# Scaling far V on ScalarE, sharing q, k copies between two engines, and a later start of the rank work, in a fused attention and shrink kernel

## The chip, the core and the metric

The kernel runs on one core of one Trainium2 chip. A core has TensorE (PE, matmuls), VectorE (DVE), ScalarE (ACT), GpSimd (POOL) and SyncE (SP), each with its own instruction stream, and 16 DMA engines that move data between device memory (HBM) and on-chip memory (SBUF). Matmul results go to PSUM, which has 8 banks. The metric is the time of one execution on the device, in microseconds (us). A profiled execution also leaves a trace of every instruction.

## The reference

There are 4 batches, 8 heads, 768 positions and 64 values a head. Some heads ("retrieval") attend to all earlier positions, the others only to the first 4 positions (sinks) and the last 64. The attention's result, 3072 rows of 512, goes through two weight matrices with a shrink between them:

```
scores = q @ k.T / 8                       # per batch and head
mask   = causal & (retrieval | sink | rel < 64)
a      = softmax(where(mask, scores, -1e9))
x      = (a @ v), heads side by side       # 3072 x 512
h      = x @ w_in                          # 512 -> 2048
out    = (h - tanh(h)) @ w_out             # 2048 -> 512
```

The data type of the matmuls is FP16, sums are FP32. Which heads are retrieval heads is data, read on the chip.

## The kernel before, in words

The 3072 rows are cut into 12 tiles of 256 rows, three a batch. A tile's q and k come in, are put in head order as FP16 (`t16`), are transposed by PE (`st_T`, line 968, four 128x128 transposes for a pair of heads) into PSUM, and copied from there to `QK` (the copies of `st_T`, lines 949 on ACT and 951 on DVE). `st_S` (line 1042) adds the masks by a matmul (line 1052, tiles 0 and 1), makes the scores (line 1063), and has ACT take the exp (line 1076) into `pt`. `st_A` (line 1156) multiplies `pt` with V; DVE divides by the row sums (lines 1176, 1203) into `x16`, and `st_X` (line 1238) transposes the result into `xT`. `H_unit` makes 256 of the 2048 hidden columns of one tile: 16 matmuls (line 1267, two halves of 8), a tanh on ACT (1279), and h - tanh(h) on DVE into `gt` (1286). `O_group` multiplies `gt` with the second matrix (1325), ACT writes the result out of PSUM (1299).

V is held in two forms. `v1` is V as it is, used for the block of 128 keys on the diagonal and the one before. Farther keys count for streaming heads only if they are sinks, so for them V is multiplied per head and key by 0 or 1 (`vf`, "far V"). For batch 0 that is done by `scale_v` (line 715): one multiply a block of 128 keys, 128 x 8 x 65, on the engine named by `SV`. Tile 0 has the blocks 0 and 1, tile 1 the blocks 2 and 3 (tile 2's keys are never far). `vf` is first read by the weighting of tile 1.

The heads of batches 1 to 3 are put in an order of ranks, retrieval heads first. `by_rank` (line 835) works the ranks out by some 15 small DVE instructions (`iota`, `prod`, `cnt`, `pos`, `perm_i`, new masks `m4r`, `mS`); POOL then reads `perm_i` into registers and gathers heads with it. The list `LATE` names data that all these small instructions, but for the masks, wait for beside their own inputs; before, it is the result of the fourth head pair of tile 0 (`x16`, 3).

The order of all instructions is set ahead by a planner (`Plan`). Each step is registered with an engine, a planned duration, what it reads and writes, and, for a DMA, its packets; `Plan.run` steps through planned time and emits, engine by engine, the ready step that was registered first. The planner also gives out PSUM banks (scores take pairs of the banks 0 to 3 in the first part, everything else single banks 4 to 7), lets up to eight POOL DMAs be outstanding, and fills planned gaps of PE early on with dummy matmuls of 128 columns (line 1482). So a changed planned duration moves instructions although nothing of the work is changed, and the order, once emitted, is fixed: an engine that waits for one instruction holds all behind it.

POOL issues in this order: V of tile 0, q and k of tile 1, V of tile 1, the four quarters of the first matrix (line 603), the first quarter of the second (614), a select that finishes a part of the mask `mS` (736), then V, q and k of tile 2 with the far V multiplies (725) between them, another quarter of the second matrix, and the raw data of tile 3.

Of the kernel before, what the change touches and what calls it, by code (L numbers as in the profile page):

```python
# [12 lines left out]
TT = 256  # L13
# [3 lines left out]
class Plan:  # L17
# [28 lines left out]
    def op(self, eng, ns, fn, r=(), w=(), dma=None, prio=None, port=False):  # L46
        i = len(self.ops)
        deps = set()
        for k in r:
            if k in self.writer:  # L50
                deps.add(self.writer[k])
            if k[0] in self.PSUM:
                deps.update(j for j in self.readers.get(k, ()) if self.ops[j][0] != eng)
            self.readers.setdefault(k, []).append(i)
        for k in w:
            if k in self.writer:
                deps.add(self.writer[k])
# [12 lines left out]
        return i  # L70
# [185 lines left out]
def kernel(  # L256
# [111 lines left out]
    ORDER = ("t1", "v1", 0, 1, 2, 3, 4, "t2", 5, "r3", 6, 7)  # L368

    def program(first):  # L370

# [111 lines left out]
        def load_v(t):  # L483

            b, g = divmod(t, NG)
            for i in range(NB):
                blk = g * NB + i
                dma(
                    "POOL", 900,
                    lambda i=i, blk=blk: nc.gpsimd.dma_start(  # L490
                        out=v1s[b]()[:, blk, :, 0:D],
                        in_=v[b, :, blk * 128 : blk * 128 + 128, :].rearrange("h p d -> p h d"),
                    ),
                    128 * H, 15.5, w=[("v1", b, blk, x) for x in range(2)],
                )

        def load_cast(t):

            b, g = divmod(t, NG)
            batch(b)  # L500
            c, ic = t16s[t] = buf("t16")
            if t >= FROM:
                c5 = lambda: c()[:].rearrange("p (i x h d) -> p i x h d", i=NB, x=2, h=H)
                for i in range(NB):
                    s0 = g * TT + i * 128
                    for x, src in enumerate((q, k)):
                        dma(
                            "POOL", 900,
                            lambda i=i, x=x, src=src, s0=s0: nc.gpsimd.dma_start(
                                out=c5()[:, i, x, :, :],  # L510
                                in_=src[b, :, s0 : s0 + 128, :].rearrange("h p d -> p h d"),
                            ),
                            128 * H, 15.5, w=[("t16", ic, x, i, s_) for s_ in range(H)],
                        )
# [5 lines left out]
            for x, src in enumerate((q, k)):  # L520
                dma(
                    "POOL", 950,
                    lambda x=x, src=src: nc.gpsimd.dma_start(
                        out=pk()[:].rearrange("p (x h e) -> p x h e", x=2, h=H)[:, x, :, :],
                        in_=src[b, :, g * TT : (g + 1) * TT, :].rearrange(
                            "h (p i) d -> p h (i d)", i=2
                        ),
                    ),
                    128 * H, 22.6, w=[("t16p", ip, x)],
                )  # L530
            if t == 1 and first:
                return
            in_order(t)
            load_v(t)

        def in_order(t):

            (pk, ip), (c, ic) = packed[t], t16s[t]
            for x in range(2):
                op(  # L540
                    "DVE", 500,
                    lambda x=x: nc.vector.tensor_copy(
                        out=c()[:].rearrange("p (x i h d) -> p x i h d", x=2, i=2, h=H)[:, x],
                        in_=pk()[:].rearrange("p (x h i d) -> p x i h d", x=2, h=H, i=2)[:, x],
                    ),
                    r=[("t16p", ip, x)] + (BEHIND if t == 1 and first else []),
                    w=[("t16", ic, x, half) for half in range(2)], port=True,
                )

        def turn(t, i):  # L550

# [166 lines left out]
        def scale_v(t, eng="POOL"):  # L718
            b, g = divmod(t, NG)
            lo = g * NB  # L720
            for jb in range(lo, min(lo + NB, 4)):
                fl = rflag0 if jb == 0 else rflag
                op(
                    eng, {"DVE": 690, "POOL": 1053}[eng],
                    lambda jb=jb, fl=fl: engs[eng].tensor_mul(
                        out=vfs[b]()[:, jb, :, :], in0=v1s[b]()[:, jb, :, :],
                        in1=fl[:].unsqueeze(2).to_broadcast([128, H, D + 1]),
                    ),
                    r=[("v1", b, jb, 0), ("v1", b, jb, 1), "rflag0", "rflag"],
                    w=[("vf", b, jb, 0)], port=True,  # L730
                )

        def select(m, src, fill, base, step, mult, key, cmp=ALU.is_ge):
# [608 lines left out]
        def visits(t):  # L1342
            g = t % NG
            gen = [t * HP + hp for hp in range(HP) if not is_near(t * HP + hp)]
            near = [t * HP + hp for hp in range(HP) if is_near(t * HP + hp)]
            if near:
                a, c = gen
                d, e = near
                return {
                    0: [[(a, 0), (d, 0)], [(c, 0), (e, 0)]],  # L1350
                    1: [[(a, 0), (a, 1)], [(d, 0), (c, 0)], [(c, 1), (e, 0)]],
                    2: [[(a, 0), (a, 1)], [(a, 2), (d, 0)], [(c, 0), (c, 1)], [(c, 2), (e, 0)]],
                }[g]
# [153 lines left out]
        def spread_over(fs, lo, hi):  # L1507
            for i, f in enumerate(fs):
                plan.setdefault(max(0, int(lo + (hi - lo) * i / max(len(fs), 1))), []).append(f)

        if first and fast:
            spread_over([by_rank], BR, BR)
        spread_over(att_pairs(1) + [lambda: scale_v(1, SV)], 0, 0)
        spread_over(attention(2), *A2)
        between = {}

        def point(h):
            t, ts = divmod(h, 2)
            return slot_of[t, 4 * ts + 3] if t >= 2 else max(0, 13 + 2 * h)
# [36 lines left out]
                spread_over(attention(t), lo, hi)  # L1556

        for s, what in enumerate(slots):
            if first and fast and s == point(2 * NG * FLEX - LEAD - 1):
                P.split = len(P.ops)  # L1560
            fs = plan.get(s, [])
            mid = (len(fs) + 1) // 2
            for i, x in enumerate(what):
                for f in fs[:mid] if i == 0 else ():
                    f()
                if x[0] == "H":
                    H_unit(*x[1:])
                else:
                    t, ts, f0, f1, c0, c1 = x[1:]
                    O_group(t, ts, f0, f1, c0, c1)  # L1570
                for f in fs[mid:] + between.get(s, []) if i == 0 else ():
                    f()
# [59 lines left out]
```

## Time and profile before

| | us |
|---|---|
| median of 3 runs | 232.07 (231.43 to 232.75) |
| the profiled execution | 233.06 |
| its span, first to last instruction | 231.3 |
| PE busy | 221.7 (96% of the span) |
| VectorE busy | 146.7 |
| ScalarE busy | 139.9 |
| GpSimd busy | 97.5 |
| mean granted TensorE clock | 0.990 |

A row of the timeline gives the start, the time to the end of the last of the instructions merged in it, the engine, the line, what is written and read, shapes, the count, and in brackets the idle time of the engine before it with what ended it. A stretch (from:to) gives its length, the busy time and count of instructions of each engine, the granted clock, the DMA share and GB/s. A busy PE isn't PE at its peak, since matmuls overlap.

### The profile page before, as it was taken

To read this page: it belongs to the slowest core of one execution; us is meant where nothing else is said; L and a number is where in the kernel's file an instruction comes from. 1 tells how busy PE (TensorE), PEld (TensorE's weight loads), DVE (VectorE), ACT (ScalarE), POOL (GpSimd) and SP (SyncE) were. 2 spreads that over 40 slices of the span, in tenths; PEclk is the share of its full clock that TensorE was granted. 3 is DMA by queue.
4 is the path that set the end of the run, shared out by engine and by line. 5 is a ranking of instruction groups with operands and counts; after the bars stand their busy time and mean duration, and the time that the engine had idled before them with its cause. 6 is when DMAs were issued, how large, how long until landed. Compare 5 with 4: busy or idle time off the path is not lost.

```text
span 231.3 us, 6135 instructions
## 1 busy us (share of the span) xinstructions
PE 221.7 (96%) x2328; PEld 158.7 (69%) x2328; DVE 146.7 (63%) x355; ACT 139.9 (60%) x214; POOL 97.5 (42%) x231
## 2 busy tenths in 40 slices
PE   7879999989999999999999999999999999999992
PEld 6446788768887666766776676765957767766652
DVE  5878887893774766755774776466867547534400
ACT  3817837975566858747547756846875867534420
POOL 8998361980281918684363968280000000000000
PEclk9988999999999999999999999999999999999999
DMA  6999999979999999999979999944121211220112
GB/s 171 150 194 206 186 223 217 208 114 204 198 202 233 195 197 233 206 198 209 248 149 252 222 250 185 212 117 114 48 45 48 60 34 45 67 47 28 48 63 80
DMA packets 102964, 35.31 MB, mean 153 GB/s; under 512 B 90642, under 2 KB 100114, under 8 KB 102930
## 3 DMA queue, kind: packets, MB, share of 16 engines
q1 hardware_dynamic: 85632, 27.14, 56.3%
q0 software_dynamic: 17152, 7.60, 25.1%
q8 instruction: 19, 0.31, 0.6%
q14 instruction: 15, 0.12, 0.2%
q10 hardware_dynamic: 146, 0.13, 0.2%
HBM read 27.26 MB, written 6.29 MB: 145 GB/s over the span
## 4 chain that ended last, share of the span: by engine, by line
PE 84%; DVE 6%; DMA 3%; POOL 2%; ACT 2%; issue 1%; POOLq 0%; DVEq 0%
PE banks L1325 36%; PE banks L1267 34%; PE banks L1063 7%; PE banks L1156 6%; DMA t16p<-in_k_dram 3%; DVE gt L1286 2%; DVE pt L1117 2%; ACT pt L1076 1%; DVE prod L846 1%; POOL v L490 1%; PE banks L968 1%; PE banks L1052 1%; ACT th L1279 1%; DVE QK L951 0%; POOL A L736 0%
## 5 line engine op out<-in xcount | busy, mean ns | idle before, releaser
L1267 PE MATMUL banks<-xT,win 128*128 128x256 f16 x768 | 95.0, 273 | 0.7 <-DVE gt L1286 0.5
L1325 PE MATMUL banks<-wout,gt 128*128 128x512 f16 (+1 forms) x464 | 94.5, 343 | 1.1 <-DVE gt L1286 1.1
L1286 DVE SCALAR_TENSOR_TENSOR gt<-th,banks 128x512 f16<-128x512 f32 x96 | 65.1, 682 | 31.5 <-ACT th L1279 30.7
L1267 PEld LDWEIGHTS <-win 128*128 128x128 f16 x768 | 72.8, 98 | 15.5 <-issue 2.1
L1279 ACT ACTIVATE th<-banks 128x512 f32<-128x512 f32 x96 | 57.1, 601 | 40.5 <-PE banks L1267 39.4
L1076 ACT ACTIVATE pt<-banks 128x768 f16<-128x768 f32 (+1 forms) x60 | 52.9, 920 | 17.3 <-PE banks L1063 16.4
L1325 PEld LDWEIGHTS <-gt 128*128 128x128 f16 x464 | 43.0, 98 | 29.3 <-DVE gt L1286 1.3
L636 POOL CAST t<-rawqk 128x256 f16 x72 | 28.6, 443 | 30.6 <-DMA rawqk<-in_k_dram 14.7
L1299 ACT ACTIVATE ot<-banks 128x512 f32<-128x512 f32 (+1 forms) x28 | 15.0, 535 | 22.0 <-PE banks L1325 21.2
L1188 DVE TENSOR_TENSOR x16t<-banks,rinv 128x128 f32 (+1 forms) x80 | 22.9, 288 | 1.8 <-DVE x16t L1188 0.2
L1099 DVE TENSOR_TENSOR ptn<-ptn,mS 128x512 f16<-128x512 f16 x24 | 10.9, 493 | 17.0 <-ACT ptn L1076 17.0
L1063 PE MATMUL banks<-QK 64*128 64x128 f16 (+1 forms) x364 | 21.4, 241 | 0.0
L672 POOL CAST v<-rawv 128x128 f16 x72 | 19.7, 320 | 0.0
L1063 PEld LDWEIGHTS <-QK 64*128 64x128 f16 x364 | 12.7, 95 | 9.9 <-issue 6.8
L1076 ACT ACTIVATE ptn<-banks 128x1024 f16<-128x1024 f32 (+1 forms) x18 | 17.2, 953 | 3.8 <-PE banks L1063 3.7
L1156 PEld LDWEIGHTS <-pt 128*128 128x128 f16 x420 | 16.3, 97 | 3.8 <-ACT pt L1076 0.7
L1156 PE MATMUL banks<-v,pt 128*128 128x65 f16 x220 | 16.6, 193 | 0.3 <-ACT pt L1076 0.2
L1127 DVE TENSOR_TENSOR pt<-pt,m4r 128x1024 f16<-128x1024 f16 (+1 forms) x18 | 12.4, 686 | 5.0 <-ACT pt L1076 5.0
L1176 DVE RECIPROCAL rinv<-banks 128x4 f32<-128x4 f32 x48 | 8.5, 177 | 8.5 <-PE banks L1156 7.7
L1156 PE MATMUL banks<-vf,pt 128*128 128x65 f16 x200 | 13.1, 193 | 0.0
L661 POOL COPY kc<-QK 128x128 f16<-128x128 f16 x12 | 3.5, 290 | 12.0 <-DMA QK<-t 11.9
L1156 PEld LDWEIGHTS <-ptn 128*128 128x128 f16 x132 | 6.4, 97 | 2.2
(79 smaller groups left out, 137.2 us busy)
## 6 DMA issues: line engine op xcount, KB each, us to landing
out_dram<-ot SPq DMA_DIRECT2D x19, 256.0 KB, 2.5
rawqk<-in_q_dram SPq DMA_DIRECT2D x18, 256.0 KB, 3.8
rawqk<-in_k_dram SPq DMA_DIRECT2D x18, 256.0 KB, 4.4
rawv<-in_v_dram SPq DMA_DIRECT2D x16, 256.0 KB, 4.6
win<-in_moe_w_in_dram POOLq DMA_DIRECT2D x4, 512.0 KB, 11.3
wout<-in_moe_w_out_dram POOLq DMA_DIRECT2D x4, 512.0 KB, 13.2
out_dram<-ot SPq DMA_DIRECT2D x9, 128.0 KB, 3.8
v<-in_v_dram POOLq DMA_DIRECT2D x6, 128.0 KB, 6.8
```

The costliest lines, as they stand in the source:

```text
L636: nc.gpsimd.tensor_copy(out=c5()[:, :, :, s_ : s_ + 1, :], in_=r5()[:, :, :, at, :])
L672: nc.gpsimd.tensor_copy(out=v1s[b]()[:, g * NB : g * NB + NB, RANK[s_] : RANK[s_] + 1, 0:D], in_=rv()[:, :, at, :],)
L1063: nc.tensor.matmul(out=sc()[:, hh, o : o + nb * 128], lhsT=lhsT, rhs=QK[p_, hp, q_0 : q_0 + nb * 128], start=not added, stop=not added or ...
L1076: lambda pt=pt, sc=sc, gi=gi, wid=wid: nc.scalar.activation(out=pt()[:, :, 512 * gi : 512 * gi + wid], in_=sc()[:, :, 0:wid], func=AF.Exp, ...
L1127: nc.vector.tensor_mul(out=pv, in0=pv, in1=m)
L1156: nc.tensor.matmul(out=av()[:, i, hh, :], lhsT=pt()[:, hh, co : co + 128], rhs=vv, start=(jb == first_jb), stop=(jb == qb),)
L1188: nc.vector.tensor_mul(out=xt()[:, :, at, :], in0=av()[:, :, hh : hh + 1, 0:D], in1=rinv()[:, :, hh : hh + 1].unsqueeze(3).to_broadcast([1 ...
L1267: nc.tensor.matmul(out=ph()[:, j, :], lhsT=w_in_t[fb // 4][:, cb, f0 : f0 + 128], rhs=xT()[:, :, cb, :], start=(cb == 0), stop=(cb == HP - 1),
L1279: lambda: nc.scalar.activation(out=th()[:], in_=ph()[:], func=AF.Tanh, scale=1.0 / XS),
L1286: lambda: nc.vector.scalar_tensor_tensor(out=gt()[:, u * FU : (u + 1) * FU, :], in0=th()[:], scalar=-XS, in1=ph()[:], op0=ALU.mult, op1=AL ...
L1299: nc.scalar.activation(out=ot()[:, c0:c1], in_=po()[:, c0:c1], func=AF.Copy, scale=1.0 / XS)
L1325: nc.tensor.matmul(out=po()[:, c0:c1], lhsT=gt()[:, f, ts * 128 : ts * 128 + 128], rhs=w_out_t[:, f, c0:c1], start=(f == 0), stop=(f == NF ...
```

## The change

There are three things that act and some that only steer the planner.

- Far V of tile 0 (`SV`) goes from GpSimd to ScalarE: for each of the two blocks, eight activations of 128 x 65 that multiply by a value per partition, one for each head, planned in pairs. Far V of tile 1 (`SV1`) stays on GpSimd.
- The eight copies of q and k of tile 1 from PSUM (`TE`, second entry), all on VectorE before, are shared: pair 0 has q on VectorE and k on ScalarE, pairs 1 and 3 q on ScalarE and k on VectorE, pair 2 both on VectorE.
- `LATE`: the small rank instructions wait for the last far V product of tile 1 (`vf`, block 3) in place of the fourth result of tile 0.
- For the planner alone: the DMAs of V and of tile 1's q are planned longer (`V1E`, `V0LAG`, `Q1E`), and every set of scores by 65 ns (160 to 225). `PARTS`, `TRI` and `SPLIT` are new, with values that leave things as they were.

```diff
-    TE = (("AA",)*4,("DD",)*4,("DD",)*4)
+    TE = (("AA",)*4,("DA","AD","DD","AD"),("DD",)*4)
-    SV = "POOL"
+    SV = "ACT"
+    SV1 = "POOL"
...
+    V1E = 17.5
+    V0LAG = 1500
+    Q1E = 37.0
+    PARTS = 1
+    TRI = ()
+    SPLIT = 1 << 30
...
-    LATE = [("x16", 3)]
+    LATE = [("vf",0,3,0)]
...
-                    128 * H, 15.5, w=[("v1", b, blk, x) for x in range(2)],
+                    128 * H, 15.5 if t > 1 or not first else V1E,
+                    w=[("v1", b, blk, x) for x in range(2)],
+                    lag=(V0LAG, 1500) if first and blk == 0 else (1100, 1500),
...
+                        128 * n, Q1E if first and t == 1 and x + part == 0 else 22.6,
...
+                if eng == "ACT":
+                    for h0 in range(0, H, 2):
+
+                        def fn(jb=jb, fl=fl, h0=h0):
+                            for h in (h0, h0 + 1):
+                                nc.scalar.activation(
+                                    out=vfs[b]()[:, jb, h, :], in_=v1s[b]()[:, jb, h, :],
+                                    func=AF.Copy, scale=fl[:, h : h + 1],
+                                )
+
+                        op("ACT", 400, fn, r=r, w=[("vf", b, jb, 0)])
+                    continue
...
-            todo, reads, keys, ns = [], [], [], 160
+            todo, reads, keys, ns = [], [], [], 225
...
-        spread_over(att_pairs(1) + [lambda: scale_v(1, SV)], 0, 0)
+        spread_over(att_pairs(1) + [lambda: scale_v(1, SV1)], 0, 0)
```

What the planner makes of it in the first 52 us: on ScalarE two of the activations stand before the second exp of tile 0, six before the third, eight after the fourth. On GpSimd the select of `mS` stands ahead of the first output-weight quarter instead of behind it, and the two multiplies left stand before the q of tile 2 and after its k. On VectorE the copy within `mS` (933) stands ahead of the q copy of tile 1 (542). On PE 12 dummy matmuls stand ahead of the first hidden unit, the first two hidden units have a set of scores between them, and two units of tile 1 stand back to back before the first transposes of tile 2.

More of the change, by code (lines that the diff above doesn't have):

```diff
@@ L519, in load_cast @@
             packed[t] = pk, ip = buf("t16p")
[L520 to L526, printed above, removed]
-                        ),
-                    ),
-                    128 * H, 22.6, w=[("t16p", ip, x)],
-                )
+            parts = PARTS if t == 1 and first else 1
+            n = H // parts
+            for part in range(parts):
+                hs = slice(part * n, part * n + n)
+                for x, src in enumerate((q, k)):
+                    dma(
+                        "POOL", 950 if parts == 1 else 780,
+                        lambda x=x, src=src, hs=hs: nc.gpsimd.dma_start(
+                            out=pk()[:].rearrange("p (x h e) -> p x h e", x=2, h=H)[:, x, hs, :],
+                            in_=src[b, hs, g * TT : (g + 1) * TT, :].rearrange(
+                                "h (p i) d -> p h (i d)", i=2
+                            ),
+                        ),
+                        128 * n, Q1E if first and t == 1 and x + part == 0 else 22.6,
+                        w=[("t16p", ip, x, half) for half in ((0, 1) if parts == 1 else (part,))],
+                    )
             if t == 1 and first:
@@ L538, in in_order @@
             (pk, ip), (c, ic) = packed[t], t16s[t]
[L539 to L548, printed above, removed]
+            parts = PARTS if t == 1 and first else 1
+            n = H // parts
+            for part in range(parts):
+                hs = slice(part * n, part * n + n)
+                halves = (0, 1) if parts == 1 else (part,)
+                for x in range(2):
+                    op(
+                        "DVE", 500 if parts == 1 else 290,
+                        lambda x=x, hs=hs: nc.vector.tensor_copy(
+                            out=c()[:].rearrange("p (x i h d) -> p x i h d", x=2, i=2, h=H)[
+                                :, x, :, hs, :
+                            ],
+                            in_=pk()[:].rearrange("p (x h i d) -> p x i h d", x=2, h=H, i=2)[
+                                :, x, :, hs, :
+                            ],
+                        ),
+                        r=[("t16p", ip, x, half) for half in halves]
+                        + (BEHIND if t == 1 and first else []),
+                        w=[("t16", ic, x, half) for half in halves], port=True,
+                    )
         def turn(t, i):
@@ L728, in scale_v @@
                     ),
[L729 to L730 removed]
+                    r=r, w=[("vf", b, jb, 0)], port=True,
                 )
@@ L1558, in program @@
         for s, what in enumerate(slots):
-            if first and fast and s == point(2 * NG * FLEX - LEAD - 1):
+            if first and fast and s == min(SPLIT, point(2 * NG * FLEX - LEAD - 1)):
                 P.split = len(P.ops)
```

10 lines of the change are left out of this document (9 added, 1 removed).

## The prediction

> **What bounds the kernel now.** I read busy time by stretches of 10 us first, then of 1 us where PE shows waits, then the timeline of the first 52 us, where everything that the change touches lies.
>
> ```profile
> span 231.3 us, 6135 instructions
> 20.00:30.00 10.00, 9.46 (x127) 7.09 (x126) 9.04 (x32) 8.12 (x12) 5.31 (x7) 1.00 1.60 191
> 60.00:70.00 10.00, 10.00 (x102) 8.99 (x101) 7.55 (x17) 5.76 (x11) 6.48 (x19) 1.00 1.17 214
> 12.00:13.00 1.00, 0.38 (x7) 0.20 (x4) 0.41 (x1) 0.29 (x1) 0.97 (x2) 1.00 2.27 166
> 14.00:15.00 1.00, 0.39 (x4) 0.17 (x4) 1.00 (x6) 0.00 (x0) 1.00 (x2) 1.00 1.31 199
> 16.00:17.00 1.00, 1.00 (x10) 0.43 (x10) 1.00 (x4) 0.00 (x0) 1.00 (x2) 0.50 1.24 207
> 21.00:22.00 1.00, 0.54 (x14) 0.33 (x9) 0.97 (x4) 0.87 (x1) 0.96 (x2) 1.00 1.24 207
> ```
>
> The columns of a stretch are length, then busy PE, weight load, DVE, ACT, POOL, granted clock, DMA. From 60 us on PE is never idle, so time is won or lost before that, and a lead then lasts to the end. Three things are to be seen: PE waits in 12 to 15, its clock is halved in 16 to 17 right after, and it waits again in 21 to 22. Meanwhile ACT is idle (0.00) and DVE full (1.00).
>
> ```profile
> 9.47 1.43 ACT L949 COPY QK<-banks 128x256 f16<-128x256 f16 x4
> 10.71 1.57 ACT L1076 ACTIVATE pt<-banks 128x768 f16<-128x768 f32 x2
> 10.92 0.68 DVE L542 COPY t<-t16p 128x1024 f16<-128x1024 f16 x1 [0.20 <-DMA t16p<-in_q_dram]
> 12.03 0.95 POOL L614 DMA_DIRECT2D wout<-in_moe_w_out_dram  x1
> 12.59 0.63 DVE L542 COPY t<-t16p 128x1024 f16<-128x1024 f16 x1 [0.99 <-DMA t16p<-in_k_dram]
> 13.03 0.34 POOL L736 TENSOR_SCALAR_AFFINE_SELECT mS<-ones 64x128 f16<-64x128 f16 x1
> 13.32 0.90 POOL L490 DMA_DIRECT2D v<-in_v_dram  x1
> 15.54 1.43 DVE L951 COPY QK<-banks 128x256 f16<-128x256 f16 x4
> 16.51 0.93 PE L1063 MATMUL banks<-QK 64*128 64x256 f16 x10
> 17.22 1.73 ACT L1076 ACTIVATE pt<-banks 128x1024 f16<-128x1024 f32 x2 [4.93 <-PE banks L1063]
> 17.78 2.30 PE L1267 MATMUL banks<-xT,win 128*128 128x256 f16 x16
> 18.69 2.49 DVE L846 TENSOR_TENSOR prod<-upto,rflag 128x64 f32<-128x64 f32 x1
> 19.02 2.07 POOL L725 TENSOR_TENSOR vf<-v,rflag 128x520 f16<-128x520 f16 x2
> 21.35 0.68 DVE L1286 SCALAR_TENSOR_TENSOR gt<-th,banks 128x512 f16<-128x512 f32 x1
> 22.08 1.47 PE L1267 MATMUL banks<-xT,win 128*128 128x256 f16 x12 [0.54 <-DVE gt L1286]
> 23.31 0.21 DVE L875 TENSOR_TENSOR prod<-pos_b,iota 128x64 f32<-128x64 f32 x1
> L603 POOL DMA_DIRECT2D win<-in_moe_w_in_dram x1: 782/782/782, 9.1 to 9.1; - x1
> DMA to landing us min/median/max: 8.6/8.6/8.6
> ```
>
> The first hidden-layer matmuls (L1267) start at 17.78 because their first weights land at 9.1 + 8.6 = 17.7: what comes earlier is free as long as it is done by then. The stall at 22.08 goes back over gt at 21.35 to one rank instruction, prod, that took 2.49 us and ended as the two POOL multiplies of far V ended (19.02 + 2.07 = 21.09).
>
> By the Trainium skill ("SBUF — State Buffer", Who interferes with whom), VectorE with two SBUF inputs and GpSimd reading SBUF share a read interface under an exclusive lock; the rows of prod and vf agree.
>
> **The change part by part.**
>
> *Far V of tile 0.* Two POOL multiplies (2.07 / 2 each) go, 16 ScalarE activations of 128x65 come: 2 ahead of the second exp of tile 0, 6 ahead of the third, 8 behind the fourth. No row shows one. The copies of 256 columns give 1.43 / 4 = 0.36, the exps of 768 give 1.57 / 2 = 0.79, so 0.84 ns a column and 0.20 us for 65 columns; the lower end is 65 x 0.84 = 0.05, the columns alone, the upper 0.38, a whole 256-column evacuation:
>
> ```profile
> L490 POOL DMA_DIRECT2D v<-in_v_dram x1: 879/879/879, 4.7 to 4.7; - x1
> DMA to landing us min/median/max: 4.5/4.5/4.5
> 51.41 0.38 ACT L1299 ACTIVATE ot<-banks 128x256 f32<-128x256 f32 x1 [0.71 <-PE banks L1325]
> ```
>
> I take 0.20, the value on the line through the two nearest kinds of row, so 3.2 us; none of them waits for its V, whose second block lands at 4.7 + 4.5 = 9.2, and behind them on ACT stand the exps and then the q, k copies. ACT's idle 4.93 us behind the tile's last exp covers the sum. The third exp slides from 10.71 to 12.3, and ACT is free at 12.3 + 3.2 = 15.5.
>
> By the Trainium skill ("ScalarE: Activation LUTs", What ACT_TABLE_LOAD costs) a per-partition scale adds about 93 ns to 186 + 0.833 N, with 93 ns overlap: an estimate of 0.24 each, 3.8 us, which no row here shows; the sum would not move, as idle time still covers it.
>
> *POOL.* DMA issues keep their order; the mask select steps ahead of the wout issue (ends at 12.4 instead of 13.37). Behind it: wout to 13.35, V of tile 2 to 14.25, far V block 2 from 14.25 to 15.3, two q, k issues (0.9 each), far V block 3 from 17.1 to 18.2. So block 3 is ready 2.9 us sooner.
>
> *Rank work.* It now waits for block 3 (18.2), hence for no POOL multiply: prod should take 0.21 instead of 2.49, as the second one does at 23.31. VectorE is 2.3 us lighter, and gt of the first unit is due 0.7 after its tanh. What queued behind prod was gt; it no longer does.
>
> *q, k of tile 1.* VectorE gets the mS copy ahead of the q copy: that waits for the select (12.4), so the q copy runs at 12.6 instead of 10.92. Two xT copies, a reciprocal (which waits for the slid exp) and the k copy follow: it ends at about 14.4 instead of 13.22. Of eight PSUM copies (1.43 / 4 each on VectorE) three go to ACT. The first pair is there at 15.7 (VectorE, behind two x16 multiplies) and 16.1 (ACT, free at 15.5), against 16.5.
>
> *PE's order.* Ahead of the first hidden unit stand 12 dummy matmuls that were not there (128 columns each, half of a hidden-layer matmul of the fence below: 0.87 / 16 = 0.054, twice that at half the clock). At full clock: scores 16.3 to 16.85, transposes 17.1, dummies 17.8, first unit 17.8: no loss. With the clock halved until 18.6 as now: masks from 16.0, scores from 16.9, first unit at 19.05. Then comes unit, scores, weighting, unit, where before both units came first:
>
> ```profile
> 68.66 0.87 PE banks L1267 x8
> 24.10 0.43 PE banks L1052 x2
> 24.53 0.49 PE banks L1063 x10
> 25.02 0.53 PE banks L1156 x14
> 31.20 1.91 PE L1325 MATMUL banks<-wout,gt 128*128 128x256 f16 x16
> ```
>
> Two units (0.87 each), one set of scores (0.92) and one weighting (0.53): 3.2 us. The third unit starts at 21.0 (full) or 22.25 (half) against 22.08. What follows to the row at 31.20 is the same work, so I arrive 1.1 early or 0.1 late.
>
> *Where the lead goes.* From 31 us the new order puts two units of tile 1 back to back ahead of the transposes of tile 2, which take over the units' PSUM banks and must wait for gt.
>
> ```profile
> 34.72 0.60 ACT L1279 ACTIVATE th<-banks 128x512 f32<-128x512 f32 x1 [3.48 <-PE banks L1267]
> 35.35 0.69 DVE L1286 SCALAR_TENSOR_TENSOR gt<-th,banks 128x512 f16<-128x512 f32 x1 [1.00 <-ACT th L1279]
> L614 POOL DMA_DIRECT2D wout<-in_moe_w_out_dram x1: 937/937/937, 21.0 to 21.0; - x1
> DMA to landing us min/median/max: 14.3/14.3/14.3
> 41.74 1.68 DVE L1117 SCALAR_TENSOR_TENSOR pt<-m,pt 128x512 f16<-128x512 f16 x2 [0.46 <-ACT pt L1076]
> 47.33 2.80 DVE L1117 SCALAR_TENSOR_TENSOR pt<-m,pt 128x512 f16<-128x512 f16 x2
> 50.98 0.83 PE L1325 MATMUL banks<-wout,gt 128*128 128x256 f16 x6 [1.06 <-DVE gt L1286]
> ```
>
> A unit that ends at 34.0 has its tanh at 34.7 and gt at 35.4: PE waits 0.7 and then 0.4 more for the second. The next output-weight quarter lands at 21.0 + 14.3 = 35.3 anyway, which eats the same lead. At 41.4 I am 0.5 ahead or 0.6 behind. Then a unit waits for a gt that stands behind a masking (1.68): 0.9 to 1.1 us against 0.4 now; I am 0.2 behind or 1.1 behind. At last the stall of 1.06 at 50.98, where gt waits behind a masking that POOL stretches (2.80), becomes one of about 0.7, since there two gts stand behind it but PE arrives later. Sum at 52 us: -0.2 (full clock) to +0.4 (half clock). Beyond 60 us PE is full and the orders differ in swaps of neighbours: zero, covered by PE's own work; if that cover fails, up to one such 1.06 stall either way.
>
> I take -0.2: nine dummies instead of five stand between the weightings in 12 to 15, the stretch whose waits cost the clock, though I hold this weakly. The profiled execution took 233.06 us (231.3 of span, 1.76 around it), 0.99 above the median 232.07; a difference found in it is applied to the median: 232.07 - 0.2 = 231.9.
>
> By the Trainium skill ("TensorE: Matmul & The Clock Gate", What's actually happening) half rate follows an idle window of about 3.4 us that runs free of the kernel's start; the trace shows the halving (0.50) after a stretch only partly idle (0.38 and 0.39 busy), and one run cannot show the phase.
>
> **The rivals.**
>
> *Faster, 230.4.* The lead is kept. The first unit starts on time, the lead at 31 us is 1.1, and the lighter VectorE (2.3 from prod, three copies of 0.36) hands gt over without the waits of 34 to 44. Then 1.1 and half of the 1.06 stall remain: 232.07 - 1.1 - 0.55 = 230.4. For it: VectorE is 9.04 busy in 20 to 30, so relief there should reach PE. Against: the 35.3 landing caps it, and the new order queues two gts behind a masking.
>
> *Slower, 233.4, by the port.* The k copy is due at 13.8 and POOL's multiply of block 2 at 14.25. If the copy starts after 14.25 it sits out the multiply to 15.3, as prod did. The transposes, scores and the first unit slide by 0.9 to 1.0: on top of the half-clock +0.4 this gives 232.07 + 1.35 = 233.4. It decides from a copy 0.45 us later than I walk it, and the reciprocal ahead of it waits for the slid exp. For it: prod's 2.49. Against: the small slide needed must come from somewhere. The lock named above is this rule.
>
> *Slower, 233.9, by ScalarE.* At 0.38 an activation ACT is free only at 12.3 + 6.1 = 18.4; the k half of the first pair then comes at 19.1, scores, transposes and dummies 1.5 later, the first unit at 20.7, 1.65 later than in the half-clock walk; with +0.4 and a little slack, +1.8. It decides above 0.25 each.
>
> **How the numbers follow.** About 0.5% (1.16 us) is what a measurement of this kernel can tell from no change. Forecast (within 0.5%, 231.3 to 232.7 with both clock cases): 0.37. Faster rival: 0.36. Port: 0.17, ScalarE: 0.10, together 0.27. So faster 0.36, same 0.37, slower 0.27, and the likeliest is 231.9. The range must take in both signs: below, a lead of 1.1 with most of the 1.06 stall gone, 230.2, leaving out about one in ten; above, the port case and a little of the ScalarE one, 233.6, leaving out one in ten.
>
> **What would show it.** Right: prod near 0.21; the vf activations near 0.20 on ACT between 8.8 and 15.5; first hidden unit at 17.8 (full clock) or 19 (half); no wait at 21 to 22; waits of PE for gt at 34 to 36, at 43 and at 50. Wrong: a k copy of over 1 us (port), the first pair of q, k copies after 17 (ScalarE), or PE without waits between 31 and 52 and every later stage over 1 us early (faster).

## The result, and the profile after

The changed kernel took a median of 234.17 us (233.23 to 236.16, 11 runs) against 231.93 (231.43 to 233.49, 11 runs) of before beside it: a ratio of 1.0092, 95% interval 1.0065 to 1.0119. It is slower by 2.2 us, outside the predicted range. The profiled execution took 234.17, the median itself, with a span of 232.3.

First the stretches of the changed kernel (columns as above), those shown of before and the three from 30 to 60 us.

```profile
core 0 of [0], span 232.3 us
12.00:13.00 1.00, 0.28 (x5) 0.10 (x2) 0.49 (x2) 1.00 (x5) 0.94 (x3) 1.00 2.33 158
14.00:15.00 1.00, 0.71 (x13) 0.41 (x10) 1.00 (x2) 1.00 (x6) 0.99 (x2) 1.00 1.26 215
16.00:17.00 1.00, 0.52 (x7) 0.22 (x5) 0.99 (x4) 0.65 (x3) 1.00 (x2) 1.00 1.24 206
20.00:30.00 10.00, 10.00 (x136) 7.64 (x135) 7.88 (x31) 8.78 (x13) 4.42 (x5) 1.00 1.59 191
30.00:40.00 10.00, 8.98 (x104) 7.43 (x101) 8.15 (x19) 4.66 (x8) 3.52 (x4) 1.00 1.26 224
40.00:50.00 10.00, 8.84 (x128) 7.01 (x127) 8.19 (x18) 9.10 (x14) 8.97 (x20) 1.00 1.24 186
50.00:60.00 10.00, 9.98 (x145) 8.54 (x145) 6.17 (x18) 6.77 (x11) 1.43 (x6) 1.00 0.83 172
60.00:70.00 10.00, 10.00 (x103) 8.99 (x101) 6.67 (x16) 5.28 (x10) 7.13 (x20) 1.00 1.11 216
```

The clock column is 1.00 everywhere: this execution was not slowed where before's profile was. TensorE waits in 12 to 17 and again between 30 and 50 (8.98 and 8.84 busy); 20 to 30 is full.

Then rows of its timeline from 11 to 63 us. Line numbers have moved: 561 is the copy into head order, 753 the new activations, 762 the far V multiply, 882 prod, 1303 the hidden units, 1361 the output matmuls, 1004 the transposes of q, k. A hidden unit is 8 matmuls (two halves of 4), as the prediction counts it, not 16.

```profile
11.11 0.27 DVE L969 COPY mS<-mS 128x128 f16<-128x128 f16 x1
11.11 1.62 ACT L753 ACTIVATE vf<-v,rflag 128x65 f16<-128x65 f16 x6
11.28 0.43 DVE L561 COPY t<-t16p 128x1024 f16<-128x1024 f16 x1
12.55 1.59 ACT L1112 ACTIVATE pt<-banks 128x768 f16<-128x768 f32 x2
13.29 0.88 POOL L497 DMA_DIRECT2D v<-in_v_dram  x1
13.88 0.18 DVE L1212 RECIPROCAL rinv<-banks 128x4 f32<-128x4 f32 x1 [1.24 <-PE banks L1192]
13.93 2.09 ACT L753 ACTIVATE vf<-v,rflag 128x65 f16<-128x65 f16 x8
13.98 1.57 DVE L561 COPY t<-t16p 128x1024 f16<-128x1024 f16 x1
14.19 1.07 POOL L762 TENSOR_TENSOR vf<-v,rflag 128x520 f16<-128x520 f16 x1
15.61 0.51 PE L1004 MATMUL banks<-ident,t 128*128 128x128 f16 x6 [0.84 <-DVE t L561]
16.82 0.45 ACT L985 COPY QK<-banks 128x256 f16<-128x256 f16 x1 [0.21 <-DVE QK L987]
17.67 1.07 POOL L762 TENSOR_TENSOR vf<-v,rflag 128x520 f16<-128x520 f16 x1
18.23 0.61 DVE L882 TENSOR_TENSOR prod<-upto,rflag 128x64 f32<-128x64 f32 x1
18.48 0.83 PE L1524 MATMUL banks<-ones 128*128 128x128 f16 x12
19.16 1.04 PE L1303 MATMUL banks<-xT,win 128*128 128x256 f16 x8
31.26 0.93 PE L1361 MATMUL banks<-wout,gt 128*128 128x256 f16 x7
35.67 0.38 PE L1004 MATMUL banks<-ident,t 128*128 128x128 f16 x4 [0.53 <-DVE gt L1322]
36.54 0.38 PE L1004 MATMUL banks<-ident,t 128*128 128x128 f16 x4 [0.49 <-DVE gt L1322]
44.81 0.38 PE L1303 MATMUL banks<-xT,win 128*128 128x256 f16 x2 [0.56 <-DVE gt L1322]
50.02 0.71 PE L1361 MATMUL banks<-wout,gt 128*128 128x256 f16 x5 [0.63 <-DVE x16t L1224]
62.93 0.60 PE L1303 MATMUL banks<-xT,win 128*128 128x256 f16 x4
```

Two things stand out. The k copy starts at 13.98, the multiply on GpSimd at 14.19, and the copy takes 1.57 instead of 0.63; the transposes wait for it (0.84 at 15.61), and the first hidden unit starts at 19.16. From 31 us on three waits for gt stand where the prediction had them, at 34 to 36 and at 44; the one at 50 is put down to `x16t`, which stood on VectorE behind a masking (48.23 to 49.76), and not to gt.

The two profiles differ by 1.0 us in span, the medians by 2.2. So I took before a second time (the first experiment below), now at full clock, and that is the trace to compare with. Its timeline, and under it two of its stretches:

```profile
core 0 of [0], span 231.4 us
12.31 0.92 DVE L542 COPY t<-t16p 128x1024 f16<-128x1024 f16 x1 [0.70 <-DMA t16p<-in_k_dram]
17.15 0.61 PE L1267 MATMUL banks<-xT,win 128*128 128x256 f16 x4 [0.36 <-DMA win<-in_moe_w_in_dram]
17.66 0.96 DVE L846 TENSOR_TENSOR prod<-upto,rflag 128x64 f32<-128x64 f32 x1
29.55 0.71 PE L1325 MATMUL banks<-wout,gt 128*128 128x256 f16 x5
60.13 0.39 PE L1267 MATMUL banks<-xT,win 128*128 128x256 f16 x2
71.75 0.34 PE L1063 MATMUL banks<-QK 64*128 64x256 f16 x4 [0.33 <-DMA QK<-t]
83.53 0.38 PE L1063 MATMUL banks<-QK 64*128 64x256 f16 x5 [0.28 <-DMA QK<-t]
105.10 0.39 PE L1267 MATMUL banks<-xT,win 128*128 128x256 f16 x2 [0.45 <-DMA xT<-x16t]
```

```profile
30.00:40.00 10.00, 9.72 (x104) 7.76 (x102) 8.04 (x20) 5.45 (x9) 3.47 (x4) 1.00 1.26 225
40.00:50.00 10.00, 9.85 (x149) 7.78 (x148) 8.24 (x18) 8.58 (x13) 9.25 (x20) 1.00 1.18 185
```

Against this trace the changed kernel is 2.0 late at the first hidden unit (19.16 for 17.15), 1.7 late at the output matmuls of tile 0 (31.26 for 29.55) and 2.8 late at the first hidden unit of tile 2 (62.93 for 60.13). Some of that is luck: the weights landed at 17.1 here and at 17.4 to 17.8 in three other traces at full clock with before's order on TensorE, which reach these marks at 29.7 to 30.2 and 60.7 to 61.1. In a fourth (21 dummies, below) they landed at 18.2, and its output matmuls would have started at 30.56. So take 0.7 to 1.7 late at 31 us and 1.9 to 2.8 at 62. Between the two marks TensorE idles 1.0 and 1.2 in after's two stretches from 30 to 50, and 0.3 and 0.15 here. And yet the span of this trace is that of the first profile, 231.4 for 231.3, though that one came to the last mark only at 62.16. What before had won by 60 us it gave back, more than half of it in waits for data that DMAs transpose (71, 83 and 105 us; the idle in the three brackets makes 1.06). The prediction had this stage as full and every lead as lasting.

### The profile page after: what moved, and what is told of

It reads as the page before. It is cut to its first block, busy times and chain, and to the rows that moved or that the text cites. A ratio compares the mean times of both kernels' runs of the same rounds, so it can differ in the third digit from the quotient of the medians.

```text
span 232.3 us, 6192 instructions
## 1 busy us (share of the span) xinstructions
PE 220.3 (95%) x2345; PEld 158.5 (68%) x2345; DVE 142.5 (61%) x352; ACT 145.5 (63%) x233; POOL 94.8 (41%) x229
## 4 chain that ended last, share of the span: by engine, by line
PE 89%; DVE 4%; ACT 3%; issue 1%; POOL 0%; POOLq 0%
PE banks L1361 36%; PE banks L1303 35%; PE banks L1099 7%; PE banks L1192 7%; ACT pt L1112 1%; DVE pt L1153 1%; PE banks L1524 1%; PE banks L1088 1%; PE banks L1004 1%; DVE t L561 1%; DVE m L862 1%; ACT QK L985 1%; DVE gt L1322 1%; ACT vf L753 1%; PE banks L1274 0%
## 5 line engine op out<-in xcount | busy, mean ns | idle before, releaser
L660 POOL CAST t<-rawqk 128x256 f16 x72 | 27.2, 424 | 28.4 <-DMA rawqk<-in_k_dram 14.9
L1135 DVE TENSOR_TENSOR ptn<-ptn,mS 128x512 f16<-128x512 f16 x24 | 10.4, 473 | 19.7 <-ACT ptn L1112 19.7
L1112 ACT ACTIVATE ptn<-banks 128x1024 f16<-128x1024 f32 (+1 forms) x18 | 17.1, 952 | 5.1 <-PE banks L1099 4.8
L1099 PEld LDWEIGHTS <-QK 64*128 64x128 f16 x364 | 12.6, 94 | 8.8 <-issue 6.6
L1163 DVE TENSOR_TENSOR pt<-pt,m4r 128x1024 f16<-128x1024 f16 (+1 forms) x18 | 11.9, 661 | 5.5 <-ACT pt L1112 5.5
L1524 PE MATMUL banks<-ones 128*128 128x128 f16 x68 | 6.3, 255 | 1.4 <-POOL ones L795 1.4
## 6 DMA issues: line engine op xcount, KB each, us to landing
wout<-in_moe_w_out_dram POOLq DMA_DIRECT2D x4, 512.0 KB, 13.8
```

Of the source, the lines that this page charges most:

```text
L660: nc.gpsimd.tensor_copy(out=c5()[:, :, :, s_ : s_ + 1, :], in_=r5()[:, :, :, at, :])
L1099: nc.tensor.matmul(out=sc()[:, hh, o : o + nb * 128], lhsT=lhsT, rhs=QK[p_, hp, q_0 : q_0 + nb * 128], start=not added, stop=not added or ...
L1112: lambda pt=pt, sc=sc, gi=gi, wid=wid: nc.scalar.activation(out=pt()[:, :, 512 * gi : 512 * gi + wid], in_=sc()[:, :, 0:wid], func=AF.Exp, ...
L1163: nc.vector.tensor_mul(out=pv, in0=pv, in1=m)
```

## The experiments

Each set ran on one chip beside before. Before's own median differed between the sets (231.93, 233.82, 233.61, 232.18, 233.13, 233.26), so only ratios within a set are compared; where two sets are, it is said. Waits in the expectations are distances from one matmul's start to the next less the usual one; the bracket of a row shows the idle part alone and is some 0.15 smaller.

**Before again, and three single edits.** The first is before unchanged.

> The kernel before, unchanged, for a trace in which TensorE's clock is not halved between 15 and 18.6 us. The profiled execution of before had that dip and took 233.06, its median is 231.93; that of after had none and took its median, 234.17. Theory: the dip costs about 1.1 us, so a trace without it has a span near 230.1, its first hidden unit still at 17.8 (its weights land then), and reaches the output matmuls of tile 0 at about 30.1 instead of 31.20. Rival: the 1.1 is spread over the span, and these matmuls start at 31.2 again.

Measured: clock 1.00, output matmuls of tile 0 at 29.55, span 231.4. The halving does cost 0.6 to 1.7 at that mark (1.0 against the trace whose weights landed at 17.8, as in the first profile), but nothing at the end: the expected 230.1 was wrong, and so was the rival's mark of 31.2.

The next was meant to part the k copy and the multiply:

```diff
                 r = [("v1", b, jb, 0), ("v1", b, jb, 1), "rflag0", "rflag"]
+                if first and eng == "POOL" and b == 0 and jb == 2:
+                    r += [("t16", t16s[1][1], 1, 0)]
```

> After, with GpSimd's multiply of far V block 2 made to wait for the k copy of tile 1 (order of every engine unchanged). Theory 1 (the k copy sits out that multiply on the shared port): the k copy takes 0.63 instead of 1.57, the first hidden unit starts 0.5 to 0.9 earlier than 19.16, and the median falls from 234.17 to 233.3 to 233.7. Theory 2 (the loss comes from the planner's new order behind 31 us): the lead is eaten by the waits for gt at 34 to 36 us, the median stays within 0.3 of 234.2.

```profile
14.00 1.54 DVE L561 COPY t<-t16p 128x1024 f16<-128x1024 f16 x1
14.17 1.07 POOL L764 TENSOR_TENSOR vf<-v,rflag 128x520 f16<-128x520 f16 x1
```

The edit did nothing: the multiply still starts under the copy. What a step names as read here moves it in planned time only; on the chip an instruction waits for the data that it touches. So this is the changed kernel a second time: 1.0021 (0.9991 to 1.0051). The same holds for `LATE`, where my account of the kernel before speaks of waiting: prod at 18.23 ran under the multiply of block 3 (17.67 to 18.74) that it was said to wait for, and took 0.61 for it, not 0.21. The change moves the rank work in the order; it adds no wait.

Without the dummies ahead of the first unit (all other steps in the same order):

```diff
-    FILL_END = 18000.0
+    FILL_END = 15000.0
```

> After, without the 12 dummy matmuls ahead of the first hidden unit (everything else in the same order). Theory 1 (the late first unit is the loss, the dummies' 0.68 us a part of it): first unit at 18.5 instead of 19.16, median 233.4 to 233.7. Theory 2 (order behind 31 us): 234.2. Rival 3: without them the clock is halved more often, 234.5 to 235.5.

Measured: first unit at 18.50, 1.0062 (1.0033 to 1.0090). The first unit came 0.66 earlier and the time rose, if anything, against 1.0021 in the same set. The clock was under 0.9955 in 3 of 12 runs against 2 of 12, which is too little to explain it. Its trace, the fastest of the 12 runs (233.82), doesn't show the loss: it is 0.6 ahead of after at 62 us (62.33 for 62.93) and ends 0.3 earlier. It stays unexplained.

The rank work alone, in before, twice:

```diff
-    LATE = [("x16", 3)]
+    LATE = [("vf",0,3,0)]
```

> Before, with the rank work alone waiting for the last far V product (the order on TensorE, ScalarE and SyncE is that of before; 26 small VectorE steps move). Theory: prod takes 0.2 to 0.6 instead of 2.49, TensorE's 0.54 of waiting at 21 to 22 us goes, and the median falls by 0.3 to 0.6, to 231.3 to 231.6. Rival: the wait only moves to a later gt, 231.9. Against both: the small instructions now stand between the gts of the next units and the time rises by 0.3 or more.

> Before with the later rank work alone, a second time (first: 0.9971, interval 0.9944 to 0.9999). If the gain of 0.3% is one, the two together exclude 1.000; if the early time is given back behind 62 us anyway, it comes out at 0.999 to 1.002.

Measured 0.9971 (0.9944 to 0.9999) and 0.9992 (0.9968 to 1.0017). Together they don't exclude 1.000, so no gain is shown. At full clock prod took 0.96 in before, not 2.49, so there was less to remove.

**The parts or the order.** For the next kernels the order of every engine and the PSUM banks are written out from the planned orders of both kernels, which register the same steps (the lists themselves are left out):

```diff
+        if self.fill:
+            order = FORCED
+            self.bank_of.update(BANKED)
+            self.size = dict(SIZED)
         for i in order:
             self.ops[i][2]()
```

> After, unchanged, beside before and the next three on one chip. First theory (the change starts the hidden units late and the rest keeps that): first unit at 19.15, 63 us where before reaches the same work at 60 to 62, ratio to before 1.005 to 1.010 as at first. Rival (what before wins early is taken back behind 60 us by transposing DMAs, so that the late start costs little): the ratio lies between 1.000 and 1.004, as the run with the unheeded wait gave (1.002).

> All three parts of the change (far V on ScalarE, the shared copies, the later rank work) in the order of before: the activations stand behind the fourth exp of tile 0, no dummies ahead of the first unit. Theory of the late start (the order, not the parts, is at fault): third exp at 10.7 and k copy at 12.3 to 13.4 as in before, first unit when its weights land (17.1 to 17.8), prod under 0.7, ratio 0.994 to 0.999. Rival (the parts cost: the copies wait on ScalarE behind the activations): first pair after 16.8, first unit after 18.3, ratio over 1.003.

> After, with its own order up to the output matmuls of tile 0 (31 us) and the order of before, written out, from there on, on every engine. Theory of the new order: the waits of 0.70, 0.65 and 0.72 at 34 to 36 and 44 us go, before's 0.4 and 1.06 come; the first hidden unit of tile 2 behind 60 us starts 0.7 earlier than in after (62.2 for 62.9), the ratio falls by 0.003. Theory of the late start: that mark stays within 0.2 of after's, and so does the ratio.

> Before, its order and engines up to the output matmuls of tile 0, and the order of after, written out, from there on. Theory of the new order: 0.7 later behind 60 us than before at the same clock (60.8 at full clock, 62.9 with the halving), ratio 1.001 to 1.004. Theory of the late start: as before, ratio 0.998 to 1.002.

| kernel (one set, before 233.61) | ratio | interval |
|---|---|---|
| after | 1.0096 | 1.0065 to 1.0127 |
| all three parts in before's order | 0.9998 | 0.9975 to 1.0022 |
| after's order to 31 us, then before's | 1.0017 | 0.9988 to 1.0046 |
| before's to 31 us, then after's | 1.0081 | 1.0046 to 1.0116 |

The three parts cost nothing by themselves. In before's order the k copy ran at 12.73, before any multiply, the first unit at 17.84 when its weights were there, and the sixteen activations filled idle time of ScalarE. What costs is the order. The late start alone costs little: followed by before's order it is taken back. The later order brings the loss back, but not by itself: where the two orders were joined, TensorE waited 1.1 us (31.13 for 30.18 with all parts in before's order), a wait that after does not have. So this kernel reaches the output matmuls as late as after does (31.26), and it too is a late start followed by the later order.

The runs of this set also list their mean granted clocks. Under 0.9955 means more than 2 us at half clock (0.0045 x 233 x 2).

| kernel | clock 0.9955 and over, median | under 0.9955, median |
|---|---|---|
| before | 233.60 (27 runs) | 233.64 (8) |
| after | 234.96 (4) | 236.26 (8) |
| after's order to 31 us, then before's | 233.73 (6) | 235.33 (4; two more took 237.6) |
| before's to 31 us, then after's | 235.04 (10) | 237.26 (2) |
| all parts in before's order | 233.85 (9) | 233.90 (3) |

A halving costs before nothing and after 1.3. Here 8 of 12 runs of after met one; in the first set 1 of 11 did, and the loss was as large. So the halving can widen the loss and is not its cause: without it after is still 1.36 behind. Nor is the loss steady between sets: in the set of the edit that did nothing, the changed kernel was 0.34 behind at that clock (234.16 for 233.82).

**Which stretch.** Before, with after's order in one stretch only.

> Before, with the order of after only between the output matmuls of tile 0 (31 us) and the seventh hidden unit of tile 1 (43 us), every engine, written out. The part to be split is the 1.0081 of after's order from 31 us on. Theory A (the two units back to back ahead of the transposes of tile 2 cost it, waits of 0.70 and 0.65 for gt): that pair of waits shows at 34 to 36 us, the first hidden unit of tile 2 comes 0.8 to 1.4 later than with before's order, ratio 1.003 to 1.006. Theory B (the waits of 0.75 at 44 and 1.1 at 50 cost it): below 1.002.

> Before, with the order of after only between 43 and 62 us. Theory B: waits of 0.75 and 1.1 for gt at 44 and 50, hidden units of tile 2 1.0 to 1.5 later, ratio 1.003 to 1.006. Theory A: below 1.002.

> Before up to 62 us, with the order of after from there on, and SyncE's whole queue in the order of after. Theory C (an early arrival at 60 us is taken back by the transposing DMAs, which in before stand behind raw loads on SyncE; in after they are issued at 65.1 instead of 66.5): TensorE's waits of 0.5 each at 71, 83 and 104 us shrink or go, ratio 0.993 to 0.998, faster than before. Rival (after's order is the worse one here too): 1.002 to 1.005.

> Before, with only SyncE's queue in the order of after (all other engines as in before). Theory C: the waits for QK at 71 and 83 us go, ratio 0.995 to 0.999. Rival (the transposes come as late, since they wait for the gather and not for the queue): 1.000 within 0.002.

Measured: 1.0053 (1.0027 to 1.0079), 1.0108 (1.0068 to 1.0148), 1.0123 (1.0088 to 1.0159), and 1.0018 (0.9990 to 1.0047) for SyncE's queue alone. The three stretches come to far more than the whole, and each mixture brought a wait of its own, which the traces of before and after don't show; one row from each of the first three:

```profile
30.79 0.38 PE L1334 MATMUL banks<-wout,gt 128*128 128x256 f16 x2 [1.17 <-DVE xT L960]
```

```profile
57.97 0.34 PE L1165 MATMUL banks<-v,ptn 128*128 128x65 f16 x6 [1.90 <-ACT ot L1308]
```

```profile
74.83 0.38 PE L1276 MATMUL banks<-xT,win 128*128 128x256 f16 x2 [1.45 <-DVE gt L1295]
```

These do not divide the loss. They tell that the orders of the queues fit each other and a mixture does not. Theory C, that SyncE's order holds the transposes back, fell: with after's queue the wait at 71 us went, one of 1.0 at 60 us came, and those at 83 and 105 us were no shorter (0.6 and 1.0).

**A slack or not, and the planner's numbers.** The delay is a loop of dummies ahead of the first output matmul (53 in the second kernel):

```diff
                 def mm(fa=fa):
+                    for _ in range(21 if first and (t, ts, fa) == (0, 0, 0) and c0 == 0 else 0):
+                        nc.tensor.matmul(
+                            out=po()[:, 0:128], lhsT=ones[:], rhs=ones[:], start=True, stop=True
+                        )
```

> Before, with 21 dummy matmuls of 128 columns (0.057 us each, 1.2 us) on TensorE ahead of the output matmuls of tile 0 at 31 us, nothing else moved. Theory F (where the clock is not halved early, before reaches 62 us some 2 us ahead of what the transposing DMAs let it use, and gives it back at 71, 83, 104 and 142 us): ratio 1.000 to 1.002. Rival P (TensorE-bound to the end, as the prediction had it, so that every delay counts in full): 1.005.

> The same with 53 dummies, 3.0 us. Theory F: the first 2 us are free where the clock is full, ratio 1.003 to 1.007, and TensorE's waits at 71, 83 and 104 us are gone. Rival P: 1.013.

Stretches of the kernel with 21 dummies, and under them those of before at full clock:

```profile
70.00:80.00 10.00, 10.00 (x105) 6.77 (x105) 5.83 (x12) 7.32 (x11) 4.49 (x12) 1.00 1.05 215
80.00:90.00 10.00, 10.00 (x111) 6.43 (x108) 6.69 (x18) 7.17 (x11) 4.50 (x16) 1.00 1.11 211
100.00:110.00 10.00, 10.00 (x83) 6.60 (x82) 5.03 (x10) 5.69 (x9) 7.17 (x21) 1.00 1.05 210
```

```profile
70.00:80.00 10.00, 9.67 (x113) 6.48 (x112) 6.47 (x15) 7.68 (x11) 5.42 (x16) 1.00 0.89 202
80.00:90.00 10.00, 9.71 (x120) 6.44 (x117) 6.60 (x17) 6.30 (x10) 4.05 (x12) 1.00 1.04 208
100.00:110.00 10.00, 9.55 (x85) 6.17 (x84) 5.03 (x12) 5.69 (x9) 6.96 (x21) 1.00 1.17 203
```

1.2 us of added work (from 30.56 to 31.73) cost nothing: 0.9980 (0.9949 to 1.0011). TensorE, late, no longer waits at 70 to 110. So before has a slack of at least 1.2 us at 31 us. 3.0 us cost 1.0125 (1.0082 to 1.0167, from 6 runs), 1.9 to 3.9 us: more than the excess over a slack, as theory F had it, and perhaps all of it. Its trace does not show how. The hidden units of tile 2 start at 62.44, no later than with 21 dummies (62.51), and yet it ends 1.8 later. TensorE waits at 126 us for a transpose (0.70), and for 0.28 and 0.31 at 136, put down to ScalarE and VectorE. The transposes of 117.9 are issued 1.6 later than with 21 dummies (116.3), but those of before at full clock came at 117.8; clearly later than there come only the ones behind a transpose at 121.47 that keeps SyncE for 2.64 us instead of 1.24 (131.2 for 129.6). Whether the delay made that DMA slow was not tested.

```diff
-    V1E = 15.5
-    V0LAG = 1100
-    Q1E = 22.6
+    V1E = 17.5
+    V0LAG = 1500
+    Q1E = 37.0
...
-            todo, reads, keys, ns = [], [], [], 160
+            todo, reads, keys, ns = [], [], [], 225
```

Before with this, and after with its reverse (the names of the first three stand in after alone, so the first kernel was made from after by setting its three parts back):

> Before, with only the planner's numbers of after (V and q planned longer, a set of scores 225 for 160), no part of the work changed. Theory O (the loss is the planner's new order, from the numbers): ratio 1.004 or more, waits for gt between 31 and 52 us of 2 us or more in all. Rival (the numbers alone do nothing, the parts make the order): within 0.002 of 1.

> After, with the planner's numbers of before: the three parts of the change, planned as before. Theory O: the order is a third one and may fall either way, but the ratio is under 1.005. Rival (the parts cost by themselves): 1.007 to 1.012, as after.

Measured: 1.0070 (1.0042 to 1.0098) for before with only the numbers changed, 1.0076 (1.0055 to 1.0097) for after with before's numbers. Either half of the change makes the planner leave the old order, and either alone costs 0.7 to 0.8%. The traces differ in where it is lost. In the first the k copy is held for 3.12 us; in the second the first unit starts at 17.09 and the output matmuls of tile 0 at 30.07, as early as in before, so the loss lies behind them. The k copies of the two:

```profile
13.05 3.12 DVE L561 COPY t<-t16p 128x1024 f16<-128x1024 f16 x1
```

```profile
14.64 0.92 DVE L561 COPY t<-t16p 128x1024 f16<-128x1024 f16 x1
```

The second expectation's theory O, under 1.005, missed; that no third order need be better was left out of it.

**The collision by itself.** The written-out order of after with one step of GpSimd's queue moved (here in words):

```diff
 V of tile 2, first block
-far V multiply, block 2
 q of tile 2
+far V multiply, block 2
 k of tile 2
```

> After, with one step moved: GpSimd's multiply of far V block 2 stands behind the issue of tile 2's q, which waits for the k copy of tile 1, so that the two cannot meet. All other queues are after's. Port theory (the prediction's first slower rival: the meeting costs 0.9 to 1.0 at the first unit and at the end): k copy 0.43 to 0.65 instead of 1.54 to 1.57, first unit at 18.2 to 18.5 instead of 19.15, ratio 0.004 lower than after's, about 1.002 to 1.005. Order theory: the k copy is as short, the first unit as early, but the output matmuls of tile 0 start within 0.3 of 31.25 and the ratio stays at 1.006 to 1.010.

```profile
core 0 of [0], span 232.1 us
14.08 0.40 DVE L570 COPY t<-t16p 128x1024 f16<-128x1024 f16 x1
14.77 0.87 POOL L545 DMA_DIRECT2D t16p<-in_q_dram  x1 [0.60 <-DVE t L570]
18.21 0.38 PE L1312 MATMUL banks<-xT,win 128*128 128x256 f16 x2
30.32 0.49 PE L1370 MATMUL banks<-wout,gt 128*128 128x256 f16 x3
62.42 0.38 PE L1312 MATMUL banks<-xT,win 128*128 128x256 f16 x2
```

Measured: 1.0026 (1.0002 to 1.0050). The copy takes 0.40, the first unit and the output matmuls come 0.95 and 0.94 earlier than in after, and none of 12 runs fell under a mean clock of 0.9955. So the collision costs 0.94 at 31 us; that is shown. At 62 us 0.51 of it is left (62.42 for 62.93), and the two profiled spans differ by 0.2. At the end it looks like 0.7% against after's 1.0092 and 1.0096, but those are other sets, and the changed kernel once came out at 1.0021 as well. No kernel here is shown to beat before.

## Why the prediction was wrong, point by point

- **Slower by the port.** This rival came true; it had 0.17. The step that failed is its condition: the copy was to collide only if it started after the multiply, at 14.25. It started 0.21 ahead, at 13.98, and was held all the same, until 0.29 after the multiply's end at 15.26. By the walk's own times, 13.8 to 14.4, it overlapped 14.25 from the outset.
- **What held the copy.** The walk left out what GpSimd did just before the multiply: it was issuing V's DMA, from 13.29 to 14.17, so the copy began under that issue. Such an issue alone holds a copy. In nine traces with before's start the k copy began 0.24 to 0.68 after the start of another issue, that of the first output-weight quarter (in before 12.03 to 12.98), and took 0.52 to 0.96 instead of 0.40 to 0.43, and each time it ended 0.25 after the issue's end; one that began 0.08 after the start of its issue took 0.43. So the likely reading is that the copy was waiting from its start, and that the multiply, which followed the issue at once, went ahead of it. The copy of 3.12 us fits: it lay under a multiply, an issue and a second multiply, and ended 0.29 after the end of the last (15.88). The one of 0.92 shows that it need not go so: it ended 0.24 after an issue's end (15.31), with the next multiply begun at 15.30. By the Trainium skill ("SBUF — State Buffer", SBUF: two separate sides) whoever starts first holds the shared ports for the whole instruction. The rows fit that if the issue counts as what started first; no run here takes the two apart.
- **The activations.** 0.20 was too low: six end 1.62 after the first starts and eight 2.09, so one follows another by (2.09 - 1.62) / 2 = 0.24. The Trainium skill's estimate ("ScalarE: Activation LUTs", What ACT_TABLE_LOAD costs) was right, my line through two other kinds of row was not. By itself it cost little: the third exp slid to 12.55 for 12.3, and the first two copies on ScalarE were done at 17.3 (16.82 + 0.45).
- **The q copy and the mS copy.** I had the latter wait for the select. It ran at 11.11, ahead of the select at 12.15, and the q copy at 11.28, not 12.6. An error without a price, as the q copy was early.
- **The first unit.** Forecast 17.8 at full clock. It was 19.16. The collision makes 0.95 of it (18.21 without) and the dummies, which I had counted as free at full clock, 0.66 (18.50 without); together that is more than the 1.36 missing.
- **Against what.** I compared marks with a profile in which the clock had been halved, and put that profile's stalls (0.54 at 22, 1.06 at 51) down to the kernel. At full clock prod took 0.96 and the output matmuls came at 29.55 to 30.56. The 1.06 comes with lateness: the kernel with 21 dummies, at full clock, has it again (at 51.33). "1.1 early or 0.1 late" was 0.7 to 1.7 late.
- **Where the lead goes.** The places of the waits, 34 to 36, 44 and 50, were right. The sizes were near at 34 to 36 (0.53 and 0.49 idle for 0.7 and 0.4) and at 50 (0.63 for 0.7, though not for gt), and too high at 44 (0.56 for 0.9 to 1.1). The walk at full clock let them cost 0.9 net of before's own (from 1.1 early to 0.2 early); between the marks at 31 and 62 us it was 0.7 against before's profile (62.93 - 31.26 less 62.16 - 31.20) and 1.1 against the trace at full clock. As a sum this step held; what it was added to did not.
- **"A lead then lasts to the end."** This failed outright. Before loses 2.0 us of lead behind 60 us, where it waits for transposing DMAs, and 1.2 us of delay cost it nothing. It was also the ground of the faster rival.
- **The clock.** That fewer waits in 12 to 15 would spare the halving is not borne out. In one set 8 of 12 runs of after were under 0.9955, and 8 of 35 of before; in another 2 of 12 of the changed kernel (with the edit that did nothing), and 13 of 29 of before.

What is shown is that the order costs, not the parts, that the collision costs 0.94 at 31 us, and that after's order from 31 us on costs behind a late start (1.0096 with it, 1.0017 with before's). That the 0.9% is the late start plus the waits of 30 to 50, less a slack of 1.2 us or more (1.9 to 2.8 late at 62 us in the traces), is argued. It fits the two kernels in which one delay alone is free: after's start with before's order, and the 21 dummies. It does not explain the kernel without dummies, nor the 1.0021 of one set, nor after with before's numbers, which passes 62 us at 62.57, where the free 21 dummies pass at 62.51, and still loses 0.8%. One guess for the 1.0021, not tested: before's medians spread over 1.9 us between sets, and its later stages wait for DMAs.

## What to carry to other kernels

Compare a profile with another of the same clock, and ask of a saved microsecond whether a later stage can use it: put a known delay there, and if it is free, so is the gain. Where a planner fixes the order, hold the order and change the parts, then the reverse; here planned numbers alone cost 0.7%. Ask of a copy on VectorE what GpSimd is doing when it starts, DMA issues included, and what it does next: here a copy that began under an issue sat out the multiply behind it.

## What had not been expected of the hardware

A VectorE copy of 0.40 us that began under a GpSimd DMA issue, 0.21 before a GpSimd multiply, took 1.57; another took 3.12, through two multiplies and the issue between them. Under an issue alone such a copy ended 0.25 after the issue's end. A halved clock early on cost before 0.6 to 1.7 us at 31 us and nothing at the end, but cost after 1.3 at the end.
